# Second layer's first round: the small products of two column streams in another order and at other places in their banks

## Chip, cores, metric

One core of a Trainium2 chip. The metric is the device time of one execution in microseconds (us). "Round" is one execution of the function `a11_round`; there are 30 in a run, one in each block of 1024 tokens but the first and the last of the 32. "Period" is the time from the start of one round to the next, from the start times in the trace; I give its median over the blocks, from which all but a few blocks differ by less than 0.01 us.

## The reference, cut

```python
# x (8, 4096, 192), weight (8, 7); w_in (192, 2048), w_out (2048, 192), all float32
w = softmax(weight)                                # per head
x = causal_conv(x, w)                              # 7 taps, per head; then (32768, 192)
h = x @ w_in
g = h * np.clip(h + 3.0, 0.0, 6.0) / 6.0
return (g @ w_out).astype(np.float32)
```

## The kernel before

A block is 1024 tokens. VectorE does the convolution of the next block, TensorE multiplies by w_in (first layer), ScalarE and VectorE form the gated values `g`, TensorE multiplies by w_out (second layer). Both layers use a Strassen scheme, which makes a product of two matrices from seven products of their quarters (A11, A12 and so on) and sums of quarters, in place of eight. In the second layer, the product A11 x B11 is again cut into seven small products of 256 tokens; this is the round. Its 32 columns of output a product fill one quarter of the array's columns, so four **column tiles** (here: tile 0 to 3) work side by side, each with a stream of its own: `m0` on tile 0 and `m1` on tile 1 (16 small products each), `m2` and `m3` on tiles 2 and 3 (8 products of 512 tokens each). A bank (`a`, `b`) is one of the eight parts of the tile `psum`, in which TensorE's results are summed.

```python
def quarters(dst, j, tokens, x, w):                # four products (u) of 256 tokens on tile j
    return [
        lambda u=u: nc.tensor.matmul(
            out=dst[rows(j), tokens], lhsT=w[:, u], rhs=x[:, u],
            start=(u == 0 and tokens == first_half), stop=(u == UNITS - 1),
            tile_position=(0, j * QS), skip_group_check=True,
        )
        for u in range(UNITS)
    ]

def a11_round(i, p1, p2):
    ...                                            # banks a and b; y, t: parts of w_out; s: sums by GpSimd
    m0 = (
        quarters(a, 0, first_half, X11, y11) + quarters(a, 0, second_half, s2, t2)
        + quarters(b, 0, first_half, s3, t3) + quarters(b, 0, second_half, X12, y21)
    )
    m1 = (
        quarters(a, 1, first_half, A12[:, ::2, first_half], w_out[:, ::2, B21, rows(2)])
        + quarters(a, 1, second_half, s1, t1)
        + quarters(b, 1, first_half, X22, t4) + quarters(b, 1, second_half, s4, y22)
    )
    m2, m3 = product(a, 2, 1, 2), product(a, 3, 2, 0)
    for n in range(NP):                            # NP = 8 steps
        for mms, k in ((m0, 2 * n), (m1, 2 * n), (m2, n), (m3, n),
                       (m0, 2 * n + 1), (m1, 2 * n + 1)):
            mms[k]()
    ...                                            # ScalarE and VectorE add up the parts of a and b
```

`A12[:, ::2]` are its chunks 0, 2, 4 and 6. Chunk 6 is the last thing that VectorE gates in a block (`UGb'` at the end of the plan of the last unit):

```python
    OTHERS = """
        UP1 UGf' LP1 URd' LGd' LP4' UP4' UGd' LF1 ... LRb' UAF LK11 UP2 URb' LGb' LP7 UP7
        URa UGb' LRa ... UK21 LGf LRd
    """.split()                                    # ' marks a step left over from the unit before
```

After the round come five groups of products on all four tiles. The second of them is short and ends with four products of 256 tokens, one on each tile:

```python
def rest_of_2(a):
    ...
    for p, tokens in ((1, slice(0, N)), (0, second_half)):
        for j in range(4):
            nc.tensor.matmul(
                out=bank[rows(j), tokens], lhsT=w[:, 2 * j + p],
                rhs=A12[:, 2 * j + p, tokens], start=bool(p), stop=True,
                tile_position=(0, j * QS), skip_group_check=True,
            )
```

Of the kernel before, what the change touches and what calls it, by code (L numbers as in the profile page):

```python
# [16 lines left out]
def kernel(  # L17
# [108 lines left out]
    w_out = cst.tile([P, NP, 8, DH], F32, name="w_out")  # L126
    B11, B12, B21, B22, T1, T2, T3, T4 = range(8)
# [157 lines left out]
    def swap(part):  # L285

        to = slice(OTHER + part.start, OTHER + part.stop)
        nc.sync.dma_start(out=y[D2:P, to], in_=y[0:D2, part])
        nc.sync.dma_start(out=y[0:D2, to], in_=y[D2:P, part])

    def y_sums():
        for o, a, b, op in (
            (YS1, OTHER, OTHER + 1, ALU.add), (YS3, OWN, OTHER, ALU.subtract),
            (YS2, YS1, OWN, ALU.subtract), (YS4, OWN + 1, YS2, ALU.subtract),
        ):
            nc.vector.tensor_tensor(out=y[:, o], in0=y[:, a], in1=y[:, b], op=op)
# [5 lines left out]
    A11, A21, A12, A22 = (g4[:, :, j] for j in range(4))  # L302
# [6 lines left out]
    def take():  # L309
        return free_banks.pop(0)  # L310

    def give(b):
        free_banks.append(b)
# [193 lines left out]
    def g_sums(engine, which, slots, width):  # L507

        forms = {
            3: (S3, A11, A21, ALU.subtract),  # L510
            2: (S2, S1, A11, ALU.subtract), 4: (S4, A12, S2, ALU.subtract),
        }
        for n in which:
            o, a, b, op = forms[n]
            for p in slots[::width]:
                r = slice(p, p + width)
                engine.tensor_tensor(out=o[:, r], in0=a[:, r], in1=b[:, r], op=op)  # L517
# [8 lines left out]
    first_half, second_half = slice(0, TH), slice(TH, N)  # L526

    X11, X12, X21, X22 = (A11[:, c::2, t : t + TH] for t in (0, TH) for c in range(2))
# [10 lines left out]
    def quarters(dst, j, tokens, x, w):  # L539
# [15 lines that stand above are left out]
        ba, bb = take(), take()  # L555
        a, b = (psum[:, n] for n in (ba, bb))
        y11, y12, y21, y22 = (
            w_out[:, k::2, B11, q * QS : (q + 1) * QS] for k in range(2) for q in range(2)
        )
        t1, t2, t3, t4 = (w_q[:, n] for n in range(4))  # L560
        s1, s2, s3, s4 = (sums[:, n] for n in range(4))
        m0 = (
            quarters(a, 0, first_half, X11, y11) + quarters(a, 0, second_half, s2, t2)
            + quarters(b, 0, first_half, s3, t3) + quarters(b, 0, second_half, X12, y21)
        )
        m1 = (
            quarters(a, 1, first_half, A12[:, ::2, first_half], w_out[:, ::2, B21, rows(2)])
            + quarters(a, 1, second_half, s1, t1)
            + quarters(b, 1, first_half, X22, t4) + quarters(b, 1, second_half, s4, y22)
        )  # L570
        m2, m3 = product(a, 2, 1, 2), product(a, 3, 2, 0)
        for n in range(NP):
# [3 lines that stand above are left out]
        mp = cs.tile([P, TH], F32, name="mp")  # L576
        r1, r2, r3 = (mp[rows(n)] for n in range(3))
        nc.scalar.copy(out=r1, in_=a[rows(0), first_half])
        piece(p1, 2, a, 2)
        piece(p2, 0, a, 3)  # L580
        add(r2, r1, a[rows(0), second_half])
        add(p1[rows(0), first_half], r1, b[rows(0), second_half])
        add(r3, r2, b[rows(0), first_half])
        add(p1[rows(0), second_half], r3, b[rows(1), first_half])
        add(p1[rows(1), second_half], r3, a[rows(1), second_half])
        add(r2, r2, a[rows(1), second_half])
        add(p1[rows(1), first_half], r2, b[rows(1), second_half])
        give(bb)
        return ba, a

    def rest_of_2(a):

        b = take()
        bank = psum[:, b]
        w = w_out[:, :, B21, rows(2)]
# [7 lines that stand above are left out]
        return b, bank  # L603

    def product(bank, j, n, q, ks=every, **tokens):
        x, w = prod[n]
        return mm(bank, j, S3 if n == 7 else x, w, q, ks, True, True, **tokens)
# [8 lines left out]
    def three(n, n4, q4):  # L616
        return four(*[(n, q) for q in range(NQ)], (n4, q4))
# [11 lines left out]
    def rows(q):  # L629
        return slice(q * QS, (q + 1) * QS)  # L630

    def piece(dst, q, src, j):
        nc.scalar.copy(out=dst[rows(q)], in_=src[rows(j)])  # L633

    def pieces(dst, q, src):
        piece(dst, q, src, 0)
        for j in range(1, 4):
            add(dst[rows(q)], dst[rows(q)], src[rows(j)])

    def add(out, x, y, op=ALU.add):  # L640
        nc.vector.tensor_tensor(out=out, in0=x, in1=y, op=op)  # L641

    def store(i, c, k, half_, qs=range(NQ), queues=(nc.sync,), tokens=slice(0, N)):

        xt = ot.tile([P, N], F32, name="xt")
        r = slice(qs[0] * QS, (qs[-1] + 1) * QS)
        nc.vector.transpose(out=xt[r, tokens], in_=c[r, tokens])  # L647
        for q in qs:
            store_rows(i, k, half_ * NQ + q, xt, q, queues[q % len(queues)], tokens)

    def sums_tiles():
        return (cs.tile([DH, N], F32, name=f"c{k}") for k in range(6))
# [50 lines left out]
    def out_strassen(i, conv):  # L703
        p1, p2, p4, p5, u2, u3 = sums_tiles()
        for u in conv:
            u()
        ba, a = a11_round(i, p1, p2)
        g_sums(nc.vector, (2,), every, 4)
        b, bank = three(4, 2, 1)
        nc.scalar.copy(out=p4[:], in_=bank[m])  # L710
        piece(p2, 1, bank, NQ)
        give(b)
        swap(slice(0, K3))
        b, bank = rest_of_2(a)
        pieces(p2, 2, bank)
        give(b)
        add(p2[rows(2), first_half], p2[rows(2), first_half], a[rows(1), first_half])
        give(ba)
        g_sums(nc.vector, (4,), every, 4)
        add(p2[:], p1[:], p2[:])  # L720
        store(i, p2, 0, 0)
        b7, bank7 = three(7, 5, 0)
        piece(p5, 0, bank7, NQ)
        y_sums()
        b, bank = three(6, 5, 1)
        piece(p5, 1, bank, NQ)
        add(u2[:], p1[:], bank[m])
        give(b)
        add(u3[:], u2[:], bank7[m])
        give(b7)  # L730
        add(p4[:], u3[:], p4[:], ALU.subtract)
        store(i, p4, 1, 0)
        b, bank = three(3, 5, 2)
        piece(p5, 2, bank, NQ)
        add(u2[:], u2[:], bank[m])
        give(b)
        add(u2[:], u2[:], p5[:])
        store(i, u2, 0, 1)
        add(u3[:], u3[:], p5[:])
        return [lambda: store(i, u3, 1, 1)]  # L740
# [18 lines left out]
    with tc.manual_schedule():  # L759
# [19 lines left out]
        b = take()  # L779
# [107 lines left out]
        for i in range(1, NB):  # L887
            h_phase(left)
            if i + 1 < NB:
                left = out_strassen(i, conv_units(i + 1, [slice(0, K3)]))  # L890
            else:
                out_last(i)
            if i + 2 < NB:
                x_tiles[i + 2] = load_x(i + 2)
# [33 lines left out]
```

## Time and profile before

| | before |
|---|---|
| time, median | 2424.14 us (3 runs, 2423.91 to 2424.36) |
| span of the profiled run | 2422.3 us |
| TensorE busy, idle | 2406.5 us, 15.8 us |
| period of a block | 74.723 us |
| largest gap between two matmul starts in a round | 0.624 to 0.629 us in 29 rounds |

The profile's lines are in the prediction. Those of TensorE's timeline in one round merge neighbouring records of one line into a row and give start, length, line and count. (A batch is, below, what starts together, about one record from each tile.) Each float32 matmul leaves two records there.

### The profile page before, as it was taken

How to read it: one execution, taken by the hardware profiler on the slowest of the kernel's cores; microseconds unless marked ns; L12 is line 12 of the kernel's file. 1: busy time of each engine (PE TensorE's matmuls, PEld its weight loads, DVE VectorE, ACT ScalarE, POOL GpSimd, SP SyncE). 2: the span in 40 equal slices, each digit the busy share in tenths (PEclk: the TensorE clock that was granted, in tenths of full speed). 3: DMA queues.
4: the chain of work that ended last, by engine and by line, in shares of the span. 5: the costliest groups of instructions: out<-in, count | busy, mean ns of one | idle time of the engine just before them, and what ended most of it. 6: DMA issues, size and time to landing. Idle time of an engine off the chain costs nothing.

```text
span 2422.3 us, 43036 instructions
## 1 busy us (share of the span) xinstructions
PE 2406.5 (99%) x17496; PEld 1105.3 (46%) x17496; DVE 2144.0 (89%) x2773; ACT 1089.2 (45%) x1858; POOL 836.5 (35%) x780
## 2 busy tenths in 40 slices
PE   9999999999999999999999999999999999999998
PEld 5444444444444444444454444444444444444443
DVE  8698889988899988899888998889998889988896
ACT  7234553345443355433454334543345443355433
POOL 2524432234422344223443224432234422344222
PEclk9999999999999999999999999999999999999999
DMA  5223333323333233333332323333323233333322
GB/s 144 48 56 61 62 62 61 66 51 70 55 60 64 52 72 61 58 58 57 67 62 57 66 55 60 62 66 58 66 51 72 53 64 59 55 69 62 58 48 45
DMA packets 261143, 149.86 MB, mean 62 GB/s; under 512 B 207504, under 2 KB 212624, under 8 KB 260944
## 3 DMA queue, kind: packets, MB, share of 16 engines
q1 hardware_dynamic: 225880, 81.56, 16.8%
q0 software_dynamic: 33824, 65.28, 15.7%
q8 instruction: 137, 2.24, 0.4%
q14 instruction: 62, 0.51, 0.1%
q10 hardware_dynamic: 1240, 0.27, 0.1%
HBM read 31.72 MB, written 25.17 MB: 23 GB/s over the span
## 4 chain that ended last, share of the span: by engine, by line
PE 96%; DVE 2%; ACT 1%; DMA 0%; issue 0%; SPq 0%; DVEq 0%; ACTq 0%
PE psum L323 51%; PE psum L456 40%; PE psum L545 4%; DVE g L333 2%; PE psum L598 1%; ACT r L329 1%; DMA x<-in_x_dram 0%; DMA out_dram<-xt 0%; DVE c L641 0%; DVE xt L647 0%; SPq L106 0%; SPq L140 0%; DVE top L184 0%; PE psum L774 0%; DVE y L275 0%
## 5 line engine op out<-in xcount | busy, mean ns | idle before, releaser
L456 PE MATMUL psum<-g,w_out 128*32 128x512 f32 (+1 forms) x7936 | 1148.2, 589 | 0.0
L323 PE MATMUL psum<-y,w_in 64*128 64x512 f32 x3664 | 885.0, 591 | 0.6 <-POOL w_in L209 0.4
L329 ACT ACTIVATE r<-psum,half 128x512 f32<-128x512 f32 x1024 | 642.0, 689 | 240.7 <-PE psum L323 233.7
L333 DVE SCALAR_TENSOR_TENSOR g<-r,psum 128x512 f32<-128x512 f32 x1024 | 641.8, 681 | 4.6 <-ACT r L329 1.5
L537 POOL TENSOR_TENSOR sums<-g 128x256 f32<-128x256 f32 x248 | 188.7, 835 | 1207.4 <-DVE g L333 1188.9
L323 PEld LDWEIGHTS psum<-y,w_in 64*128 64x128 f32 x3664 | 433.1, 187 | 373.8 <-issue 296.6
L456 PEld LDWEIGHTS psum<-g,w_out 128*32 128x32 f32 x7936 | 329.8, 110 | 445.8 <-issue 436.1
L323 PE MATMUL psum<-y,w_in_t 64*128 64x512 f32 x1984 | 524.4, 592 | 0.0
L415 DVE TENSOR_TENSOR psum<-psum,p 128x512 f32<-128x512 f32 x496 | 324.6, 694 | 195.8 <-PE psum L323 186.9
L633 ACT COPY c<-psum 32x512 f32<-32x512 f32 x218 | 126.3, 579 | 588.0 <-PE psum L456 577.2
L517 POOL TENSOR_TENSOR s<-g 128x1024 f32<-128x1024 f32 x124 | 293.7, 2368 | 244.2 <-PE psum L323 236.4
L275 DVE SCALAR_TENSOR_TENSOR y<-x,c_sb,y 128x1536 f32<-128x1536 f32 (+1 forms) x206 | 366.3, 1784 | 6.6
L323 PEld LDWEIGHTS psum<-y,w_in_t 64*128 64x128 f32 x1984 | 247.3, 186 | 194.3 <-issue 125.0
L517 DVE TENSOR_TENSOR g<-g 128x2048 f32<-128x2048 f32 x124 | 279.5, 2296 | 7.3 <-DMA g<-g 3.8
L456 PE MATMUL psum<-s,w_out 128*32 128x512 f32 x1488 | 230.3, 592 | 0.0
L408 ACT COPY psum<-psum 128x512 f32<-128x512 f32 x248 | 138.8, 571 | 72.4 <-PE psum L323 57.6
L641 DVE TENSOR_TENSOR c<-c,psum 32x512 f32<-32x512 f32 (+2 forms) x219 | 140.8, 643 | 31.4 <-ACT c L633 25.1
L443 POOL DMA_DIRECT2D g<-g x124 | 149.1, 1202 | 39.8 <-POOL s L517 39.8
L411 ACT COPY p<-psum 128x512 f32<-128x512 f32 x248 | 133.2, 590 | 40.5 <-PE psum L323 39.8
L545 PE MATMUL psum<-g,w_out 128*32 128x256 f32 x720 | 132.6, 382 | 6.9 <-DVE g L333 6.9
L456 PEld LDWEIGHTS psum<-s,w_out 128*32 128x32 f32 x1488 | 73.7, 110 | 131.7 <-issue 124.3
L545 PE MATMUL psum<-sums,w_q 128*32 128x256 f32 x720 | 109.2, 380 | 0.0
(64 smaller groups left out, 1097.7 us busy)
## 6 DMA issues: line engine op xcount, KB each, us to landing
g<-g POOLq DMA_DIRECT2D x124, 512.0 KB, 5.0
out_dram<-xt SPq DMA_DIRECT2D x380, 64.0 KB, 2.0
y<-y SPq DMA_DIRECT2D x62, 384.0 KB, 4.9
x<-in_x_dram SPq DMA_DIRECT2D x55, 388.5 KB, 6.0
stage<-in_moe_w_in_dram SPq DMA_DIRECT2D x16, 192.0 KB, 4.5
stage<-in_moe_w_out_dram SPq DMA_DIRECT2D x8, 384.0 KB, 5.3
x<-in_x_dram SPq DMA_DIRECT2D x7, 384.0 KB
y<-y SPq DMA_DIRECT2D x6, 128.0 KB, 2.4
```

What stands on the lines that cost most here:

```text
L275: nc.vector.scalar_tensor_tensor(out=to, in0=x[:, part, k + t : k + t + W], scalar=c, in1=to, op0=ALU.mult, op1=ALU.add,)
L323: nc.tensor.matmul(out=psum[:, b], lhsT=w[r], rhs=y[r, third_of_y], start=start, stop=stop, skip_group_check=onto,)
L329: nc.scalar.activation(r6, h, ACT.Relu, bias=half[:], scale=1.0 / 6.0)
L333: nc.vector.scalar_tensor_tensor(out=out, in0=r6, scalar=1.0, in1=h, op0=ALU.min, op1=ALU.mult)
L408: nc.scalar.copy(out=psum[:, bank["b"]], in_=psum[:, bank["a"]])
L415: nc.vector.tensor_tensor(out=psum[:, to], in0=psum[:, bank["b"]], in1=self.p5[:], op=ALU.add)
L443: nc.gpsimd.dma_start(out=S1[:, slots], in_=A22[:, slots], accum_op=ALU.add)
L456: lambda p=p: nc.tensor.matmul(out=bank[j * QS : (j + 1) * QS, tokens], lhsT=w_out[:, p, w, cols], rhs=x[:, p, tokens], start=(first and p ...
L517: engine.tensor_tensor(out=o[:, r], in0=a[:, r], in1=b[:, r], op=op)
L537: nc.gpsimd.tensor_tensor(out=o, in0=a, in1=b, op=op)
L545: lambda u=u: nc.tensor.matmul(out=dst[rows(j), tokens], lhsT=w[:, u], rhs=x[:, u], start=(u == 0 and tokens == first_half), stop=(u == UN ...
L641: nc.vector.tensor_tensor(out=out, in0=x, in1=y, op=op)
```

## The change

The intent is to ask later for what comes late: A12's even chunks go from the first to the second quarter of `m1`, the sums of GpSimd to later quarters, and products whose inputs are ready early (X22, X12) forward. Banks and places follow the order, and the additions after the round follow the places. Nothing is added or taken away.

```diff
@@ -560,13 +560,13 @@
         t1, t2, t3, t4 = (w_q[:, n] for n in range(4))
         s1, s2, s3, s4 = (sums[:, n] for n in range(4))
         m0 = (
-            quarters(a, 0, first_half, X11, y11) + quarters(a, 0, second_half, s2, t2)
-            + quarters(b, 0, first_half, s3, t3) + quarters(b, 0, second_half, X12, y21)
+            quarters(a, 0, first_half, X11, y11) + quarters(a, 0, second_half, X12, y21)
+            + quarters(b, 0, first_half, s2, t2) + quarters(b, 0, second_half, s3, t3)
         )
         m1 = (
-            quarters(a, 1, first_half, A12[:, ::2, first_half], w_out[:, ::2, B21, rows(2)])
-            + quarters(a, 1, second_half, s1, t1)
-            + quarters(b, 1, first_half, X22, t4) + quarters(b, 1, second_half, s4, y22)
+            quarters(a, 1, first_half, X22, t4)
+            + quarters(a, 1, second_half, A12[:, ::2, first_half], w_out[:, ::2, B21, rows(2)])
+            + quarters(b, 1, first_half, s1, t1) + quarters(b, 1, second_half, s4, y22)
         )
         m2, m3 = product(a, 2, 1, 2), product(a, 3, 2, 0)
         for n in range(NP):
@@ -578,12 +578,12 @@
         nc.scalar.copy(out=r1, in_=a[rows(0), first_half])
         piece(p1, 2, a, 2)
         piece(p2, 0, a, 3)
-        add(r2, r1, a[rows(0), second_half])
-        add(p1[rows(0), first_half], r1, b[rows(0), second_half])
-        add(r3, r2, b[rows(0), first_half])
-        add(p1[rows(0), second_half], r3, b[rows(1), first_half])
-        add(p1[rows(1), second_half], r3, a[rows(1), second_half])
-        add(r2, r2, a[rows(1), second_half])
+        add(p1[rows(0), first_half], r1, a[rows(0), second_half])
+        add(r2, r1, b[rows(0), first_half])
+        add(r3, r2, b[rows(0), second_half])
+        add(p1[rows(0), second_half], r3, a[rows(1), first_half])
+        add(p1[rows(1), second_half], r3, b[rows(1), first_half])
+        add(r2, r2, b[rows(1), first_half])
         add(p1[rows(1), first_half], r2, b[rows(1), second_half])
         give(bb)
         return ba, a
@@ -714,7 +714,7 @@
         b, bank = rest_of_2(a)
         pieces(p2, 2, bank)
         give(b)
-        add(p2[rows(2), first_half], p2[rows(2), first_half], a[rows(1), first_half])
+        add(p2[rows(2), first_half], p2[rows(2), first_half], a[rows(1), second_half])
         give(ba)
         g_sums(nc.vector, (4,), every, 4)
         add(p2[:], p1[:], p2[:])
```

## The prediction

> **What bounds the kernel now.** I read the page first, then the waits of TensorE, then the timeline of one round of the second layer. Parts 1 and 4 of the page:
>
> ```profile
> PE 2406.5 (99%) x17496; PEld 1105.3 (46%) x17496; DVE 2144.0 (89%) x2773; ACT 1089.2 (45%) x1858; POOL 836.5 (35%) x780
> ...
> PE 96%; DVE 2%; ACT 1%; DMA 0%; issue 0%; SPq 0%; DVEq 0%; ACTq 0%
> ```
>
> TensorE is busy 99% of the span and is 96% of the chain that ended last; the granted clock is at its top in all 40 slices. A change that removes no matmul can therefore gain only what TensorE spends waiting, and the page leaves 2422.3 - 2406.5 = 15.8 us of idle, part of it start and end. The waits of TensorE say where it sits in the steady part:
>
> ```profile
> PE psum L545 <- DVE g L333: 6.9, 29, 0.2
> PE psum L782 <- DVE half L254: 1.5, 1, 1.5
> PE psum L323 <- POOL w_in L209: 0.4, 1, 0.4
> ```
>
> Line 545 is the helper of the small products (256 tokens wide), so in the steady part there is one wait, in 29 of the 30 rounds, each time on the gating operation of VectorE. 6.9 us is not its cost, though, because matmul ends in this profile are modelled. The timeline of TensorE in the round that starts at 1034.56 us shows the start times, which I trust more:
>
> ```profile
> 1034.80 0.60 PE L545 MATMUL psum<-g,w_out 128*32 128x256 f32 x4
> 1035.03 0.60 PE L456 MATMUL psum<-g,w_out 128*32 128x512 f32 x2
> 1035.23 0.60 PE L545 MATMUL psum<-g,w_out 128*32 128x256 f32 x4
> 1035.46 0.60 PE L456 MATMUL psum<-g,w_out 128*32 128x512 f32 x2
> 1035.67 0.59 PE L545 MATMUL psum<-g,w_out 128*32 128x256 f32 x3
> 1035.89 0.60 PE L456 MATMUL psum<-g,w_out 128*32 128x512 f32 x2
> 1036.10 0.38 PE L545 MATMUL psum<-g,w_out 128*32 128x256 f32 x1
> 1036.72 0.40 PE L545 MATMUL psum<-g,w_out 128*32 128x256 f32 x1 [0.24 <-DVE g L333]
> ```
>
> Every matmul leaves two records here. Batches of line 545 start 0.43 us apart, and single starts alternate about 0.22 us apart (1035.67, 1035.89, 1036.10). The next should have started at 1036.10 + 0.21 or 0.22 = 1036.31; it started at 1036.72. So the wait costs **0.41 us** a round, of which the profile calls 0.24 idle. In the trace's start times the gap is 0.624 to 0.629 us in the 29 rounds, against a regular 0.216: again 0.41.
>
> What it waits for is seen on VectorE, in the timeline of the same stretch:
>
> ```profile
> 1031.58 5.09 DVE L333 SCALAR_TENSOR_TENSOR g<-r,psum 128x512 f32<-128x512 f32 x8
> 1036.59 1.81 DVE L271 TENSOR_SCALAR y<-x,c_sb 128x1536 f32<-128x1536 f32 x1
> ```
>
> The eight last gates end at 1031.58 + 5.09 = 1036.67, and TensorE goes on 0.05 us later. By the kernel's plan for the last unit the eighth gate is the upper half's result "b", which is chunk 6 of A12. The second stream of the round starts with A12's even chunks (0, 2, 4, 6) in the first 256 tokens, two of its 16 small products to each of the eight steps; chunk 6 is its fourth product, the last of step 1. Code and times name the same product.
>
> **What the Trainium skill says.** "Perfetto Trace Analysis", section "Tensor Engine Instruction (MATMUL, LD_WEIGHTS)", has the end of a matmul record as an estimate and the wait for semaphores outside the record. The trace agrees: 0.24 us is called idle where the starts show 0.41 lost. "Perfetto Trace Analysis", section "Optimization Strategy", says to find gaps on the limiting engine, find which instruction ends them, and make that dependency start sooner; this change does the mirror of that, asking for the data later. "TensorEngine Tiling (Array Packing)", section "Key Properties", says a change of tiling mode drains TensorE while changes of tile do not. The trace agrees: from the 64x128 tiles of the first layer to the 128x32 tiles of the round the start gap is 0.519 us against a regular 0.429, in every round. The change keeps all tile positions, so it stays. "PSUM — Partial Sum Buffer", section "The four PSUM rules", allows the first-matmul flag only on the first group in a bank and quadrant; both orders keep it on the first-half groups, which still come first, so no instruction for zeroing is added.
>
> **The change part by part.** It removes and adds no instruction: still 16 products in each of two streams, same widths, same two banks and column places, one ACT copy and eight VectorE additions (one of them later, into p2). Their cost is unchanged: 30 rounds of 32 small products at the same cadence, and about 0.41 us for an addition of 32x256. What moves:
>
> 1. A12's even chunks go from products 1-4 to products 5-8 of their stream. With two a step and a step of 0.86 us (two records, 2 x 0.43), chunk 6 is wanted at the end of step 3, not of step 1: 2 x 0.86 = 1.73 us later. From the round's start at 1034.56 it was due at 1036.31, and is now due at 1038.04; the data is there at 1036.72. Slack: 1.3 us. Gain 0.41 us a round.
> 2. X22 with t4 takes the early place. Its last chunk, 7, second token half, comes from the lower half's gate "f", third of the eight: ready at 1031.58 + 3 x 0.64 = 1033.5, due at 1036.3. No wait.
> 3. X12 with y21 goes from products 13-16 of the first stream to 5-8, and its last chunk is from that same gate (first token half). No wait.
> 4. s2, s1 move from the second place to the third; s3 from the third to the fourth; s4 stays last. GpSimd ends s2 at 1035.03 + 0.86 = 1035.89, s1 and s3 before, s4 at 1035.96 + 0.73 = 1036.69; they are due from 1038 on. These waits are already free today; the move only adds slack.
> 5. The additions after the round take other places but wait for the whole round in effect: VectorE does its 13.3 us of convolution first and comes to them at 1049.95, with the round over at 1042.36. No change.
>
> Sum: 29 rounds x 0.41 = 11.9 us. The thirtieth, at 1259.1 us, is an experiment that nature made. There TensorE came 0.35 us late (the period before is 75.075 us, against 74.72 as a rule, the one after 74.375), the round was 0.35 us shorter, and the wait was some 0.06 us:
>
> ```profile
> 1260.62 0.68 PE L545 MATMUL psum<-g,w_out 128*32 128x256 f32 x2
> 1260.90 0.40 PE L545 MATMUL psum<-sums,w_q 128*32 128x256 f32 x1
> ```
>
> It shows that VectorE's date holds, whatever TensorE does, and that the rest of the block runs at TensorE's own pace. It adds 0.06 us. Together **12.0 us**: 2424.1 - 12.0 = 2412.1 us, 0.5%.
>
> **What lies behind it.** The gain lasts only if TensorE, 0.41 us earlier after the round, meets no VectorE result that does not move. VectorE has no idle from 1031.58 to about 1071.4, so its dates in the second layer stay. S2's first half is ready at 1053.03 + 2.25 = 1055.3 and wanted from 1056.96: slack 1.7 becomes 1.3. S4's first half is ready at 1060.16 + 2.25 = 1062.4 and wanted at about 1063.9: 1.5 becomes 1.1. The first sum of y is ready at 1065.93 + 0.65 = 1066.6 and wanted about 1072.2. VectorE's next wait is for ACT's copy of the last big product at 1071.96, where it sat idle 0.56 us; it moves 0.41 us earlier with TensorE, so the next block's gates move along. Idle there becomes 0.15 us: VectorE is close, not yet the bound.
>
> **Rivals.** (a) The wait turns into another: a sum of GpSimd, or the third stream (A12 times B21 in the same chunk order), which meets chunk 6 at step 6, near 1039.7 us. For it speaks only that everything arrives in the same microseconds; the dates in points 1 to 4 speak against it. Time: 2418 with half the gain lost, 2424 with all. (b) VectorE becomes the bound: busy 67.0 of the block's 74.73 us, with idle mostly in the first layer (1.8 to 2.0 us a unit). If some bank or gate there holds TensorE up, a part of 0.41 us is given back each block: 2414 to 2420. Against it: idle of VectorE there ends with TensorE, not the other way round. (c) The gain is far larger, since the chain has DVE 2% and ACT 1% (3% is over 70 us). It can't be: in the round's part of the chain ACT's 0.68 us and VectorE's 1.30 us lie beside matmuls from 1034.56 to 1036.31, so that 1.6 of the 2 us are filled. If TensorE were really waiting there: 2360.
>
> **Range and chances.** 2412.1 by the sum. Some tenths of a us in a few blocks, as in the odd round, can come on their own (0.35 each); rivals (a) and (b) pull up, hardly anything pulls down. I take 2409.5 to 2416.5. Same within 2% (over 2375.7 and under 2472.6): 0.985; faster 0.01; slower 0.005.
>
> **What would show each step.** In the profile of the changed kernel: the row of line 545 waiting for the gate is gone from TensorE's waits; the largest start gap within the round is 0.22 to 0.25 us, and its small products take about 7.17 us first to last start, not 7.58; the period of a block is 74.31 us; the chain has nearly no DVE g and ACT r; VectorE's idle before the addition at the end of the block is about 0.15 us. Wrong would be: a row in which TensorE waits for GpSimd's sums, or line 456 for the gate, of about 0.2 us 29 times; or an unchanged period though the gap is gone, with a new gap in lines 323 or 456.

## The result, and the profile after

| | before | after |
|---|---|---|
| time, median of 4 runs | 2424.02 us | 2399.21 us (2398.86 to 2399.28) |
| TensorE busy | 2406.5 us | 2388.7 us |
| TensorE idle | 15.8 us | 8.4 us |
| period of a block | 74.723 us | 73.866 us |

The ratio of the fast runs is 0.9897 (95% interval 0.988 to 0.9914), so the time is the same within 2%. The change saves 24.8 us; 12.0 were predicted, and the time lies outside the range of 2409.5 to 2416.5. Of the signs named in advance, the row of line 545 is gone and the largest gap in the round is 0.220 us, as said; the small products take 6.72 us from first to last start and not 7.17, and the period is not 74.31.

Parts 1 and 4 of the page of the changed kernel, busy time and the chain that ended last:

```profile
PE 2388.7 (100%) x17496; PEld 1105.0 (46%) x17496; DVE 2138.0 (89%) x2773; ACT 1087.9 (45%) x1858; POOL 836.4 (35%) x780
...
PE 99%; DMA 0%; DVE 0%; SPq 0%; ACT 0%; issue 0%; DVEq 0%; ACTq 0%
```

The number of matmul records is the same, and yet TensorE is busy 17.8 us less. Busy time of TensorE here counts a moment in which one of four tiles works the same as one in which all four do. So the 15.8 us of idle before, which I took for the most that could be gained, was no bound.

TensorE's waits after; the row of line 545 is gone, as predicted:

```profile
PE psum L782 <- DVE half L254: 1.5, 1, 1.5
PE psum L323 <- DVE y L275: 0.3, 1, 0.3
PE psum L323 <- POOL w_in L209: 0.2, 1, 0.2
```

The timeline of TensorE in one round after, which starts at 1023.96 us. The stretch is the one that the prediction shows for the kernel before, 0.88 to 1.54 us after the start:

```profile
1024.84 0.38 PE L545 MATMUL psum<-g,w_out 128*32 128x256 f32 x1
1024.85 0.38 PE L545 MATMUL psum<-g,w_q 128*32 128x256 f32 x1
1024.85 0.60 PE L456 MATMUL psum<-g,w_out 128*32 128x512 f32 x2
1025.06 0.38 PE L545 MATMUL psum<-g,w_out 128*32 128x256 f32 x1
1025.07 0.38 PE L545 MATMUL psum<-g,w_q 128*32 128x256 f32 x1
1025.28 0.38 PE L545 MATMUL psum<-g,w_out 128*32 128x256 f32 x1
1025.28 0.59 PE L456 MATMUL psum<-g,w_out 128*32 128x512 f32 x1
1025.28 0.38 PE L545 MATMUL psum<-g,w_q 128*32 128x256 f32 x1
1025.29 0.59 PE L456 MATMUL psum<-g,w_out 128*32 128x512 f32 x1
1025.49 0.38 PE L545 MATMUL psum<-g,w_out 128*32 128x256 f32 x1
1025.50 0.38 PE L545 MATMUL psum<-g,w_q 128*32 128x256 f32 x1
```

Because the two streams now read different tensors, they can be told apart: `w_out` is tile 0, `w_q` is tile 1 (X22 with t4). Tile 1's fourth product has its two records at 1025.28 and 1025.50, that is 1.326 and 1.542 us after the start of the round (here and below unrounded start times, medians over the rounds). In the kernel before, the same place shows three records of line 545 where there should be four (the row "x3" at 1035.67) and then one alone at 1036.10. Both missing records are those of tile 1; the trace didn't lose them, as each round has its 64 records of line 545. Its fourth product, A12's chunk 6, was due 1.326 us after the start and began at 2.160. **Tile 1 lost 0.834 us**. The 0.41 us that I read is the time from the next regular start of tile 0 to 2.160, and that is what tiles 0, 2 and 3 lost. They lost it because their next products, due at about 1.75, stand behind chunk 6 in the program: the start times show that products behind one that waits for data don't start either. (In `tile3_early` below, where the waiting product stands earlier, tile 0's next product, due at 1.319, begins at 2.166.)

The end of the second layer shows that the difference stayed. The last rows of line 456 and the first of the first layer, before, in the block that starts at 1034.56:

```profile
1070.28 0.99 PE L456 MATMUL psum<-g,w_out 128*32 128x512 f32 x3
1071.21 1.13 PE L323 MATMUL psum<-y,w_in 64*128 64x512 f32 x4
```

And after, in the block that starts at 1023.96:

```profile
1059.19 0.62 PE L456 MATMUL psum<-g,w_out 128*32 128x512 f32 x4
1059.74 1.13 PE L323 MATMUL psum<-y,w_in 64*128 64x512 f32 x4
```

After, the last batch is four records that start within 0.04 us and take 0.62 us together. Before, three records take 0.99 us: by the start times the last batch of four begins 35.69 us after the start of the round, the row shows its last two, and one more record follows alone at 36.12, some 0.4 us behind. One tile works by itself for a batch while three are done and wait for the change of tiling mode.

The sum: 0.834 us lost at the start, and 0.024 us more because the first step of tile 1 after the wait takes 0.240 us and not 0.216. That is 0.858 us, and the periods differ by 74.723 - 73.866 = 0.857 us. Thirty times that is 25.7 us. Some 1.0 us is given back (see the point on VectorE below), which leaves 24.7; 24.8 was measured. That the change of tiling mode makes the tiles wait for the latest was not tested by moving it. What speaks for it is that in all twelve kernels the first layer starts 0.52 us after the last record of the latest tile, be it tile 1 or, in `tile3_early`, tile 3.

### The profile page after: what moved, and what is told of

Read it like the earlier page. It is cut to its first block, busy times and chain, and to the rows that moved or that the text cites. A ratio compares the mean times of both kernels' runs of the same rounds, so it can differ in the third digit from the quotient of the medians.

```text
span 2397.1 us, 43036 instructions
## 1 busy us (share of the span) xinstructions
PE 2388.7 (100%) x17496; PEld 1105.0 (46%) x17496; DVE 2138.0 (89%) x2773; ACT 1087.9 (45%) x1858; POOL 836.4 (35%) x780
## 3 DMA queue, kind: packets, MB, share of 16 engines
q0 software_dynamic: 33824, 65.28, 15.8%
## 4 chain that ended last, share of the span: by engine, by line
PE 99%; DMA 0%; DVE 0%; SPq 0%; ACT 0%; issue 0%; DVEq 0%; ACTq 0%
PE psum L323 51%; PE psum L456 41%; PE psum L545 5%; PE psum L598 2%; DMA x<-in_x_dram 0%; DMA out_dram<-xt 0%; DVE c L641 0%; DVE xt L647 0%; SPq L106 0%; SPq L140 0%; DVE top L184 0%; PE psum L774 0%; DVE y L275 0%; SPq L95 0%; ACT y L788 0%
## 5 line engine op out<-in xcount | busy, mean ns | idle before, releaser
L456 PE MATMUL psum<-g,w_out 128*32 128x512 f32 (+1 forms) x7936 | 1120.0, 589 | 0.0
L323 PEld LDWEIGHTS psum<-y,w_in 64*128 64x128 f32 x3664 | 441.6, 187 | 362.6 <-issue 292.2
L456 PEld LDWEIGHTS psum<-g,w_out 128*32 128x32 f32 x7936 | 339.4, 110 | 460.3 <-issue 438.1
L456 PE MATMUL psum<-s,w_out 128*32 128x512 f32 x1488 | 218.9, 592 | 0.0
L545 PE MATMUL psum<-g,w_out 128*32 128x256 f32 x720 | 109.4, 380 | 0.0
```

Of the source, the lines that this page charges most:

```text
L323: nc.tensor.matmul(out=psum[:, b], lhsT=w[r], rhs=y[r, third_of_y], start=start, stop=stop, skip_group_check=onto,)
L456: lambda p=p: nc.tensor.matmul(out=bank[j * QS : (j + 1) * QS, tokens], lhsT=w_out[:, p, w, cols], rhs=x[:, p, tokens], start=(first and p ...
L545: lambda u=u: nc.tensor.matmul(out=dst[rows(j), tokens], lhsT=w[:, u], rhs=x[:, u], start=(u == 0 and tokens == first_half), stop=(u == UN ...
```

## The experiments

**Theory A**: what counts is how late a product starts against the due time of its own tile. The tile stays that late, as the four streams run separately, until the change of tiling mode at the end of the layer, where all wait for the latest. **Theory B**: the prediction's loss of 0.41 us on the engine as a whole was right, and another part of the change (order or places of some other product) is worth as much again. All times of before below are from the same rounds on the same chip: medians of 2423.91, 2423.94 and 2424.01 us in the three groups.

### One stream alone

`m1_only` has the new `m1` and the old `m0`; `m0_only` the reverse. The additions follow the places in each.

```diff
 m1_only, against the changed kernel
-    quarters(a, 0, first_half, X11, y11) + quarters(a, 0, second_half, X12, y21)
-    + quarters(b, 0, first_half, s2, t2) + quarters(b, 0, second_half, s3, t3)
+    quarters(a, 0, first_half, X11, y11) + quarters(a, 0, second_half, s2, t2)
+    + quarters(b, 0, first_half, s3, t3) + quarters(b, 0, second_half, X12, y21)
 m0_only, against the kernel before
-    quarters(a, 0, first_half, X11, y11) + quarters(a, 0, second_half, s2, t2)
-    + quarters(b, 0, first_half, s3, t3) + quarters(b, 0, second_half, X12, y21)
+    quarters(a, 0, first_half, X11, y11) + quarters(a, 0, second_half, X12, y21)
+    + quarters(b, 0, first_half, s2, t2) + quarters(b, 0, second_half, s3, t3)
```

> The second stream (column tile 1) as in the changed kernel, so A12's chunks later; the first stream (column tile 0) in its old order. Theory A (tile's own stream): the wait cost column tile 1 not 0.41 us but 0.83 us, from 1.326 us after the round's start, when its fourth product was due by the start times of the changed kernel, to 2.160, when it started; the four column tiles run on as separate streams, so tile 1 stays behind until the change of tiling mode at the end of the second layer. Then this kernel has the whole gain: block period 73.87 us, time 2399 us. Theory B (the engine's gap of 0.41 us, as predicted, and as much again from another part of the change): 2412 us if the other part is the order of the first stream, 2399 us if it is in the second.

> The first stream as in the changed kernel, the second with A12 first as before. Theory A: nothing gained, 2424 us, period 74.72 us, gap of 0.62 us in each round. Theory B: up to half of the gain, 2412 us, if the order and places of the first stream are worth something by themselves.

Measured: `m1_only` 2399.54 us, period 73.864; `m0_only` 2423.98 us, period 74.722, with the old gap. All of the gain is in the second stream. The first stream's order, and with it the later place of s2 and s3, is worth nothing.

### One product alone, moved by two places and by one

```diff
 chunk6_two_later, against the kernel before
+    m1.insert(5, m1.pop(3))
 chunk6_one_later, against the kernel before
+    m1.insert(4, m1.pop(3))
```

> The kernel before with one product alone moved: A12's chunk 6 goes from the fourth to the sixth place of the second stream, all banks and places in the banks as before. Theory A: due at about 2.19 us after the round's start, data at 2.16, so no loss to speak of: 2399 to 2400 us, period 73.87 to 73.9. Theory B: the wait is gone, worth 0.41 us a round, the rest of the change is missing: 2412 us.

> The kernel before with A12's chunk 6 moved by one place only, fourth to fifth of the second stream. Theory A: due at about 1.76 us after the round's start, data at 2.16, so 0.40 us of the 0.83 stay: 2411 us, period 74.27, and a gap of some 0.4 to 0.6 us still to be seen in the start times. Theory B: due at 2.18, no wait and no gap to be seen, 2412 us, period 74.31. So here the gap, not the time, tells them apart.

Measured: two places later 2399.69 us, period 73.867. One product out of 48 in the round carries the whole gain; banks and places of the kernel before were fine. One place later: 2411.11 us, period 74.292. There chunk 6 began at 2.160 us against a due time of 1.758, 0.402 us late. The period is 0.426 us above the changed kernel's, which is 0.402 and the 0.024 of the restart. The gap that I expected to see, 0.4 to 0.6 us, isn't there: tile 0 still had a record at 1.967, so no two starts of the round are more than 0.22 us apart (the drain before it left out), and TensorE's waits have no row of line 545. That part of the expectation failed, and it was the sign that I had fixed to tell the theories apart: by it, this run would go to B. What speaks for A here, the start 0.402 us late, I read only afterwards, so the other runs have to decide. If they do, the case against reading gaps gets stronger: 0.43 us a round, some 12 us in all, with no gap and no wait to be seen.

### The data earlier by one gate

```diff
 gate_swap, against the kernel before
-    PLANS = [FIRST, SECOND] + [OTHERS] * (UNITS - 1)
+    LAST = "UGf' URd' LGd' LP4' UP4' UGd' URb' LRb' UGb' LGb'".split()
+    PLANS = [FIRST, SECOND] + [OTHERS] * (UNITS - 2) + [LAST]
```

> The kernel before with the last two gates (and their activations) of a block exchanged, so that chunk 6 of A12 is ready one gate, 0.64 us, earlier: at about 1.52 us after the round's start. Theory A: tile 1 was due at 1.326, so 0.19 us of the 0.83 stay: gain 0.64 us a round, 2405 us, period 74.06. Theory B: due at 1.75, so nothing is left of the 0.41 us and no more is gained: 2412 us, period 74.31.

Measured: 2407.23 us, period 74.145. That is between the two expectations, and nearer to A's 2405 than to B's 2412. Chunk 6 began at 1.581 us, not at 1.52: I had taken 0.64 us for a gate, but in the kernel before the last two end 0.596 us apart (1.510 and 2.106), and here the seventh ends 0.016 later, at 1.526; the product follows 0.055 later. So tile 1 was 0.255 us late; with the restart that makes 0.279, and the period is 74.145 - 73.866 = 0.279 above the changed kernel's. Theory B has no loss at all here, as TensorE's waits have none:

```profile
PE psum L783 <- DVE half L254: 1.5, 1, 1.5
PE psum L323 <- DVE y L275: 0.3, 1, 0.3
PE psum L323 <- POOL w_in L209: 0.2, 1, 0.2
```

The streams can be seen apart in the timeline of a round of this kernel, which starts at 1027.75 us (the helper is line 546 here):

```profile
1029.28 0.45 PE L546 MATMUL psum<-g,w_out 128*32 128x256 f32 x2
1029.50 0.38 PE L546 MATMUL psum<-sums,w_q 128*32 128x256 f32 x1
1029.50 0.60 PE L457 MATMUL psum<-g,w_out 128*32 128x512 f32 x2
1029.57 0.38 PE L546 MATMUL psum<-g,w_out 128*32 128x256 f32 x1
```

Tiles 0, 2 and 3 go on at their old cadence (1029.50), and tile 1 (w_out of line 546) runs 0.07 us behind a start of tile 0, at 1029.57, and on at that distance. It was due at 1.542 + 1027.75 = 1029.29 with that record. No tile but the late one has lost anything. Tile 1's next product begins at 2.036 us, after products of tiles 2 and 3 (1.754 and 1.761) that stand behind it in the program. So a product that waits for its data holds up what stands behind it on all tiles, as in the kernel before, but one that waits for its own busy tile doesn't hold up the others.

### Is it one tile that sets the end?

These take the 256-token product of tile 1, or of tile 2, out of the short group behind the round (`rest_of_2`). Their outputs are wrong, which doesn't matter for the times.

```diff
 drop_tile1, drop_tile2 (2 in place of 1), after_drop_tile1 (the same on the changed kernel)
         for j in range(4):
+            if not p and j == 1:
+                continue
             nc.tensor.matmul(
```

> The kernel before without one small product (256 tokens, two records of 0.216 us) of column tile 1 in the batch behind the round (wrong result on purpose). Theory A: tile 1 alone is 0.43 us behind the three others, so leaving out 0.43 us of its own work lets it catch up: period 74.72 - 0.42 = 74.30, time about 2411.5 us. Theory B: four tiles run side by side and three still have the product, so nothing changes: 2424 us.

> The same product left out on column tile 2 (wrong result on purpose). Theory A: tile 2 isn't the late one, nothing gained: 2424 us, period 74.72. Theory B: as with tile 1, 2424 us. If instead any product left out gains 0.1 to 0.4 us a block, theory A's picture of one late tile is wrong.

> The changed kernel without the 256-token product of column tile 1 behind the round (wrong result on purpose). Theory A: no tile is late any more, so three others still set the end: nothing gained, 2399 us. If leaving it out gains here too, some 0.4 us a block or 12 us, then tile 1 is the longest stream for another reason than the wait, and theory A's reading of the same experiment on the kernel before is wrong.

Measured: without tile 1's product 2412.79 us, period 74.329 (0.394 us less, 0.42 expected); without tile 2's 2424.07 us, period 74.723; on the changed kernel without tile 1's 2399.29 us, period 73.859. The same 0.43 us of work is worth 0.39 us on tile 1 behind a wait, and nothing on another tile or without the wait. The end of the layer in `drop_tile1` has the full last batch again:

```profile
1065.99 0.63 PE L456 MATMUL psum<-g,w_out 128*32 128x512 f32 x4
1066.55 0.70 PE L323 MATMUL psum<-y,w_in 64*128 64x512 f32 x2
```

The second form of this gives half of that product (128 tokens) to tile 2 and keeps the result right:

```diff
 rebalanced, against the kernel before
-    for p, tokens in ((1, slice(0, N)), (0, second_half)):
-        for j in range(4):
-    ...
+    work = [(1, j, j, slice(0, N)) for j in range(4)] + [(0, 0, 0, second_half)]
+    quarter = slice(TH, TH + TH // 2), slice(TH + TH // 2, N)
+    work += [(0, 1, 1, quarter[0]), (0, 2, 2, second_half)]
+    work += [(0, 3, 3, second_half), (0, 1, 2, quarter[1])]
+    for p, c, j, tokens in work:           # chunk 2 * c + p on tile j
+    ...
```

> The kernel before with half of that product (128 of 256 tokens) given from tile 1 to tile 2; right result. Theory A: tile 1 is 0.83 behind by the wait and gets 0.21 back, 0.62; tile 2 is 0.42 behind and gets 0.21 more, 0.63: gain 0.20 us a block, 2418 us. Theory B: tile 2 has 0.21 us more than the others, so 0 to 0.21 us a block lost: 2424 to 2430 us.

Measured: 2418.46 us, period 74.539, 0.184 us less than before. A kernel with one matmul more in each block is faster, because the late tile has less to do.

### Another tile made late

```diff
 tile3_early, against the changed kernel
-    m2, m3 = product(a, 2, 1, 2), product(a, 3, 2, 0)
+    m2, m3 = product(a, 2, 1, 2), product(a, 3, 2, 0, (0, 6, 1, 2, 3, 4, 5, 7))
```

> The changed kernel, with the order of the eight chunks in its fourth stream (A12 times B21, 512 tokens, column tile 3) changed from 0..7 to 0, 6, 1, 2, 3, 4, 5, 7, so that chunk 6 is its second product. By the changed kernel's start times that product is due 0.903 us after the round's start; the data is there at 2.16. Theory A (lateness against the tile's own due time, kept to the end of the layer): 1.26 us a round lost, period 75.12 us, time about 2437 us, slower than the kernel before. Theory B (the engine's gap, counted from the last start before the wait): last start 1.325, next regular start about 1.54, so 0.62 us lost, 2418 us.

Measured: 2435.93 us, period 75.120. The product began at 2.159 us, 1.256 after its due time of 0.903; the period rose by 1.254. The row of the wait in this kernel:

```profile
PE psum L456 <- DVE g L333: 7.0, 29, 0.2
```

The kernel before had 6.9 us in such a row and lost 0.857 us a round; this one has 7.0, and lost 1.254. `chunk6_one_later` and `gate_swap` have no row and lost 0.426 and 0.279. (All against the period of the changed kernel.) The row says that there is a wait. It says nothing of its price.

## Why the prediction was wrong, point by point

**The step that failed** is the size of the wait: "The next should have started at 1036.10 + 0.21 or 0.22 = 1036.31; it started at 1036.72. So the wait costs 0.41 us a round". The mechanism was right: the gate, chunk 6, the fourth product of the second stream and the cure by a later place are all confirmed by `gate_swap` and `chunk6_two_later`. The term was mis-sized. I took the wait from the engine's next regular start, as if TensorE were one queue in which any start answers for all. The product that waited was due not at 1036.31 but at 1034.56 + 1.326 = 1035.89, in one batch with three records that did start. It lost 0.834 us, and with the restart 0.858. I had the evidence in the fence: x4, x4 and then x3 and x1. I read the start times and not the counts.

**The experiment that nature made** was misread in the same way. In the odd round chunk 6 began at 1.812 us, so tile 1 was still 0.486 us late, not 0.06. The start times show what had happened before: in the first layer of that block, one of its two row streams fell 0.353 us behind, from about 60.3 us after the start of its block (the one that starts at 1184.01), and stayed so to the end of the layer while the other kept its time to 0.002 us. (A row stream here: the products on one of the two tiles of 64 rows, 64*128 in the trace.) An addition of VectorE (line 415) came first: it started at 58.94 us against 58.59 in other blocks; nothing in the trace says why. VectorE's date did hold, as I said; but the 0.35 us came off a wait of 0.834, not off one of 0.41. It is the same thing as on tile 1, in the other tiling mode.

**The ceiling** was wrong: "can gain only what TensorE spends waiting, and the page leaves 2422.3 - 2406.5 = 15.8 us". The gain was 24.8. An idle tile beside a busy one isn't in that number.

**Rival (c)** was dismissed with the wrong argument. The chain's 2% DVE and 1% ACT were indeed too much (over 70 us), but the reason I gave, that matmuls filled the time up to 1036.31, holds for three tiles and not for the one that the chain went through. In rival (a), the stream with A12 times B21 is the fourth (`m3`), not the third; its time of 1039.7 us is right.

**Points 2 to 5** held in their effect: no new wait appeared in the round, the first stream's moves gave nothing (`m0_only`), and the additions cost the same (0.41 us before and after). No instruction was added: 17496 matmul records both times. Slack of the moved chunk was overstated: by its own tile it is due four products later, at 1.326 + 4 x 0.432 = 3.05 us, so 0.9 us and not 1.3.

**What lies behind it** came out as feared, in small. I had VectorE's idle at the end of a block going from 0.56 to 0.15 us; as the gain was 0.86 and not 0.41, it went to nothing. VectorE's addition of the last big product, before and then after (in the block whose next round starts at 728.5 us):

```profile
1071.96 0.68 DVE L641 TENSOR_TENSOR c<-c,psum 96x512 f32<-96x512 f32 x1 [0.56 <-ACT c L633]
```

```profile
691.46 0.64 DVE L641 TENSOR_TENSOR c<-c,psum 96x512 f32<-96x512 f32 x1
```

There is no idle before it now, and in that block the weight loads of the first layer wait for VectorE a little later:

```profile
PEld psum L323 <- DVE psum L415: 0.3, 1, 0.3
```

The period of that block is 74.033 us, 0.17 over the rule. Four of the 29 periods are longer by 0.14 to 0.17 us, at the same place in the first layer, one row stream behind and the other not; I looked at the wait in one of them. They are the blocks in which VectorE was already behind before the change: its second step of the convolution, 3.87 us after the start of the round, takes 2.54 to 2.60 us there, in both kernels, and 2.16 to 2.25 in the others. Before, that left 0.205 to 0.239 us of VectorE's idle of 0.56; after, the addition comes 0.3 us later than in the other blocks. A fifth, 74.217, is the odd block's 0.35 us, which used to vanish in the round's wait and no longer does. Together that is 1.0 us given back. Rival (b) was right in kind, at 0.6 us in all. Why that step is longer in just those four blocks (every sixth), and what causes the odd one, stays open.

**Chances**: "within 2%" was right; the range was too narrow. Only 2.6 of its 7.0 us lay below the sum, and no rival stood for a wait some tenths of a us larger than I had read it.

No experiment points to a kernel faster than the changed one: `m1_only`, `chunk6_two_later` and it lie within 0.5 us of each other.

## What to carry to other kernels

Where TensorE runs several tiles side by side, follow each tile's stream by itself: take the due time of a late product from its own tile's cadence (or from a kernel in which it isn't late), and count records in a batch rather than look for gaps. A tile that falls behind stays behind up to the next point where all tiles meet, so a late input belongs late in its stream, and work taken off the late tile before that point is worth nearly the same as that much of the wait (here 0.39 us for 0.43 us of work). When sizing a wait, a row in the waits proves that there is one, but neither its time nor its absence says what it costs.

## What the Trainium skill lacked or had wrong

- "Perfetto Trace Analysis", section "Optimization Strategy", has one look for gaps between slices on the limiting engine. With column tiles that isn't enough: `gate_swap` lost 0.279 us a round and `chunk6_one_later` 0.426 with no two starts in the round more than 0.22 us apart (0.24 in one round of `gate_swap`) and no row among TensorE's waits.
- "Perfetto Trace Analysis", section "Identifying the Most-Contended Engine", warns against matmul busy time and offers MFU (the share of the peak rate of arithmetic) and the busy share of weight loads. The warning is borne out: busy fell 17.8 us with the same 17496 records. The other two divide by the whole time, so they follow it (weight loads 1105.3 us before and 1105.0 after, 45.6% and 46.1%) but don't show that a tile waits, or where.
- "TensorEngine Tiling (Array Packing)", section "Key Properties", says tiles operate independently and a change of mode drains the engine. Both agree with the runs (`gate_swap`; the 0.52 us above). What is missing is what follows from the two together: a tile 0.834 us late in the round was still one batch (0.43 us) behind the others some 34 us later, and the drain made all wait for it. Nor does it give a size for the drain itself: here 0.519 us between starts against 0.429, so 0.09 us at the change from the first layer's tiles to the second's.
- No page that I found has the restart of a stream: the first step of a tile after a wait took 0.240 us in place of 0.216 with 256-token products.
